# Chunked linear attention in front of a two-layer pair: eight heads to a step instead of four, two accumulator banks for the first product, and the split of the weights on another engine

## Chip, cores and metric

The kernel runs on one core of one Trainium2 chip. The metric is the device time of one execution in microseconds; three runs of the kernel before gave a median of 1195.69 us (1194.02 to 1195.76). TensorE is PE in the tables (its weight loads PEld), VectorE is DVE, ScalarE is ACT, GpSimd is POOL, SyncE is SP and issues the DMAs.

## Reference

The inputs q, k and v have 4 batches, 8 heads, 768 positions and 64 features. The weights are two pairs of a 512 x 2048 and a 2048 x 512 matrix. All of it is float32 for the result; the weights reach the chip as float64 words.

```python
gamma = 1.0 - 2.0 ** (-5.0 - np.arange(H, dtype=np.float32))
for t in range(S):
    state = gamma[None, :, None, None] * state + np.einsum('bhd,bhe->bhde', k[:, :, t], v[:, :, t])
    y[:, :, t] = scale * np.einsum('bhd,bhde->bhe', q[:, :, t], state)
x = y as 3072 tokens x 512
h = x @ w_in;  x = np.maximum(0.01 * h, h) @ w_out        # first pair
h = x @ w_in2; out = np.where(h > 0, h, exp(min(h, 0)) - 1) @ w_out2   # second pair
```

## The kernel before, in words

The 3072 tokens are 24 chunks of 128 positions (six to a batch) and 6 blocks j of 512 tokens (four chunks to a block). The hidden width 2048 is 16 slices m of 128. A step is one slice for one block. It consists of a first product h = w_in[m] x (L225, 12 matmuls), the nonlinearity on ACT (`leaky`, L304), its split into a high and a low part (`split_g`: ACT L231, then DVE or POOL L232), and a second product into four accumulators y (L246, 12 matmuls, issued two steps later by `drain`). Each product is three matmuls per operand pair, since every operand is held as a rounded high part and a remainder (hi·hi, hi·lo, lo·hi). There are 96 steps for each of the two pairs, so 384 blocks of 12 matmuls. Their order is written out by hand in `VISITS` (L46): block 0 with slices 0 to 3, block 1 with slices 0 to 7, block 0 with the other 12, block 1 with the other 8, then whole blocks. A visit that does not finish its 16 slices stores its accumulators to memory, and the later visit adds them (`drain`, L270 to L280).

Attention works on units of half a chunk, four heads (`att_a`, `att_b`; 48 units). One unit does: scores sc = k·q (L357), a mask product to SBUF on DVE (pt, L363 and L365), then into one bank o the state part st·q (L382), pt·v (L385) and the state's increment k·v (L389); ACT copies the output to xhi (L392), DVE updates the state st (L398, two instructions, or L401) and writes the remainder xlo (L402). POOL scales k and q by the decay tables (`prep_k` L333, `prep_q` L342). These matmuls are plain float32, and the profile shows each as two records, so a unit has eight records for each of the four kinds. `att_step` (L418) issues the scores of the next unit and the outputs of the present one together. Eight units stand ahead of the first step, two go with each of the next four steps, then they are spread thinly over blocks 2 to 5's waiting time.

PSUM has eight banks: y takes four, h one, the scores two, o one. One unit in two of the first four chunks uses the y banks instead.

The first pair's weights arrive as 16 loads of 1 MB in 64-bit words (`load_w`) and are converted in the kernel, one slice at a time, by a list of operations (`conv_ops`): ACT takes the top 16 bits out (`put`, L93), DVE masks them twice (`c_exp`, L96 and L97), ACT rebiases the exponent (L100), DVE builds the mantissa (`c_top` L103, `c_low` L107), joins the sign (`c_sign` L111) and multiplies (`c_mul` L114). Then `c_split` rounds to the high part on ACT and forms the remainder on POOL (`halves`, L117 and L118). `conv(n)` issues the next n of these operations; the loop over steps (L461) says how many. The second pair's weights are converted during blocks 2 to 5 in the same way by `pre`, and go through memory.

All DMAs are issued by SP in program order. The first ones are chunk 0, the tables, weight 0, then chunks 1 to 5 with weights 1 to 3 between them. Inside the loop a step issues the load of chunk c+2 and of the next weight.

```python
# the loop of a step, shortened
gemm1(0, m, j % 2, h); conv(n1); gf = leaky(h)
if n > 2: att_step(3 if s < 2 else 2)
else: c_split()
split_g(s, gf, nc.gpsimd if vi < 2 else nc.vector, gp, 3)
drain(s - 2, ...); conv(n2)
if n > 2: att_step(1, 1)
```

Of the kernel before, what the change touches and what calls it, by code (L numbers as in the profile page):

```python
# [19 lines left out]
F32 = mybir.dt.float32  # L20
# [11 lines left out]
P = 128  # L32
# [20 lines left out]
def body(ctx: ExitStack, tc: tile.TileContext, kkv, w1, w2, tabs, out):  # L53
# [19 lines left out]
    raw, wt, cvt, exps, ready = {}, {}, {}, [], []  # L73
# [42 lines left out]
    def halves(hi, lo, f):  # L116
        nc.scalar.copy(hi, f)  # L117
        nc.gpsimd.tensor_tensor(lo, f, hi.bitcast(F32), ALU.subtract)  # L118

# [23 lines left out]
    def c_mul(i):  # L143
        e, _, f = cvt.pop(i)
        power(e, f)
        ready.append((i, f))

    def c_split():
        if ready:
            i, f = ready.pop(0)  # L150
            t = wt[0, i] = wp.tile([P, 2 * W], F32R, tag=f"w{i}", name="w")
            halves(t[:, :W], t[:, W:], f)

    def conv_ops():
        yield c_put, 0
        for i in range(MF):
            yield c_exp, i
            yield c_top, i
            yield c_low, i
            yield c_sign, i  # L160
            if i + 1 < MF:
                yield c_put, i + 1
            yield c_mul, i

# [28 lines left out]
    def pre(more):  # L193
# [20 lines left out]
        halves(r[:, :BLK], r[:, BLK:], f)  # L214
# [93 lines left out]
    with ExitStack() as actx:  # L308
# [4 lines left out]
        st = ab.tile([P, NP, D], F32, name="st")  # L313
        tab = ab.tile([P, H * C + NP * C + 2 * H], F32, name="tab")
        ktab = tab[:, :H]
        mask = tab[:, H : H + H * C].rearrange("p (i r t) -> p i r t", i=2, r=2)
        qtab = tab[:, H + H * C : H + H * C + NP * C].rearrange("p (a t) -> p a t", a=NP)
        gtab = tab[:, H + H * C + NP * C :]
# [10 lines left out]
        def prep_k(w):  # L329
            c, i = divmod(w, 2)  # L330
            if c < NCH and c % NCB < NCB - 1:
                k = kv[c][:, 2, 4 * i * D : 4 * (i + 1) * D].rearrange("p (h d) -> p h d", h=4)
                nc.gpsimd.tensor_tensor(k, k, ktab[:, 4 * i : 4 * i + 4].unsqueeze(2).to_broadcast([P, 4, D]), ALU.mult)  # L333

        qd = {}

        def prep_q(w):
            c, i = divmod(w, 2)
            if c < NCH and c % NCB:
                qd[w] = ap_.tile([P, 2, C], F32, tag="qd", name="qd", bufs=3)  # L340
                q = kv[c][:, 1, 2 * i * C : 2 * (i + 1) * C].rearrange("p (a t) -> p a t", a=2)
                nc.gpsimd.tensor_tensor(qd[w], q, qtab[:, 2 * i : 2 * i + 2, :], ALU.mult)  # L342

        def att_a(w):


            c, i = divmod(w, 2)
            if w < 2 * CPB and i:
                sc = [ps.tile([P, 2 * C], F32, tag=f"y{r}", name="sc") for r in range(2)]
            else:  # L350
                both = aps.tile([P, 2, BLK], F32, tag="s", name="sc")[:, :, : 2 * C]
                sc = [both[:, r] for r in range(2)]
            for p in range(2):
                a = slice((2 * i + p) * C, (2 * i + p + 1) * C)
                for r in range(2):
                    rs = slice(r * D, (r + 1) * D)
                    nc.tensor.matmul(sc[r][:, p * C : (p + 1) * C], kv[c][rs, 0, a], kv[c][rs, 1, a], start=True, stop=True,  # L357
                                     skip_group_check=True)
            yield
            t = ap_.tile([P, 2, 2 * C], F32, tag="pt", name="pt")  # L360
            if w < 2 * CPB and i:
                for r in range(2):
                    nc.vector.tensor_tensor(t[:, r], sc[r], mask[:, i, r], ALU.mult)  # L363
            else:
                nc.vector.tensor_tensor(t, both, mask[:, i], ALU.mult)  # L365
            pt[w] = t
            yield

        def att_b(w):

            c, i = divmod(w, 2)
            cb = c % NCB
            t = pt.pop(w)
            if w < 2 * CPB and i:
                o = ps.tile([P, 2, 2, C], F32, tag="y2", name="o")
            else:
                o = aps.tile([P, 2, 2, C], F32, tag="o", name="o")
            pairs = [(p, 2 * i + p, r, slice(r * D, (r + 1) * D)) for p in range(2) for r in range(2)]
            if cb:
                q = qd.pop(w)  # L380
                for p, a, r, rs in pairs:
                    nc.tensor.matmul(o[rs, p, 0, :], st[rs, a, :], q[rs, p, :], start=(p == 0), stop=False, skip_group_check=True)  # L382
            for p, a, r, rs in pairs:
                v = kv[c][:, 3, a * C + r * D : a * C + (r + 1) * D]
                nc.tensor.matmul(o[rs, p, 0, :], v, t[:, r, p * C : (p + 1) * C], start=(cb == 0 and p == 0), stop=True, skip_group_check=True)  # L385
            if cb < NCB - 1:
                for p, a, r, rs in pairs:
                    hs = slice(a * C + r * D, a * C + (r + 1) * D)
                    nc.tensor.matmul(o[rs, p, 1, :D], kv[c][:, 2, hs], kv[c][:, 3, hs], start=False, stop=True, skip_group_check=True)  # L389
            b, ts = c // CPB % 2, slice(c % CPB * C, (c % CPB + 1) * C)  # L390
            ks = slice(2 * i, 2 * i + 2)
            nc.scalar.copy(xhi[b][:, ks, ts], o[:, :, 0, :])  # L392
            yield
            if cb < NCB - 1:
                if cb:
                    for p in range(2):
                        a = 2 * i + p
                        nc.vector.scalar_tensor_tensor(out=st[:, a, :], in0=st[:, a, :], scalar=gtab[:, a : a + 1],  # L398
                                                       in1=o[:, p, 1, :D], op0=ALU.mult, op1=ALU.add)
                else:  # L400
                    nc.vector.tensor_copy(st[:, ks, :], o[:, :, 1, :D])  # L401
            nc.vector.tensor_tensor(xlo[b][:, ks, ts], o[:, :, 0, :], xhi[b][:, ks, ts].bitcast(F32), ALU.subtract)  # L402
            yield

        NU = 2 * NCH
# [5 lines left out]
        load_w()  # L411
        nc.sync.dma_start(out=tab[:, cut:], in_=tabs[:, cut:])
        for c in range(1, CPB + 2):
            att_load(c)
            if c != 2 and c < CPB + 1:
                load_w()

        def att_step(before=0, between=0):  # L418


            nonlocal au
            w = au
            c, i = divmod(w, 2)
            scores = att_a(w + 1) if w + 1 < NU else iter((0, 0))
            outputs = att_b(w)
            next(scores)
            conv(before)
            next(scores)
            prep_q(w + 2)
            next(outputs)  # L430
            conv(between)
            next(outputs)
            prep_k(w + 1)
            c_split()
            if i and CPB <= c < NCH - 2:
                att_load(c + 2)
            au += 1
# [7 lines left out]
        au = 0  # L445
# [4 lines left out]
        for _ in att_a(0):  # L450
            pass
        for w, (n1, n2) in enumerate(((0, 1), (0, 1), (1, 0), (1, 1), (0, 1), (1, 1), (0, 1), (1, 1))):
            att_step(n1, n2)
            if w < 2:
                warm(1)


        units = {0: 4, 3: 2, 4: 1, 5: 1, 6: 1}
        pace = {1: (2, 2), 2: (2, 1)}
        NA = next(s for s, (_, j, _, _) in enumerate(steps) if j == NB - 1)  # L460
        for s in range(NA):  # L461
            ph, j, m, (_, _, m0, m1, vi) = steps[s]
            n = units.get(vi, 0)
            h = ps.tile([P, BLK], F32, tag="h", name="h")
            gemm1(0, m, j % 2, h)
            n1, n2 = pace.get(vi, (0, 0))
            conv(n1)
            gf = leaky(h)
            if n > 2:
                att_step(3 if s < 2 else 2)  # L470
            else:
                c_split()
            split_g(s, gf, nc.gpsimd if vi < 2 else nc.vector, gp, 3)
            drain(s - 2, stage_w if vi < 2 or m < m0 + 2 and vi == 2 else stage_f)
            conv(n2)
            if n > 2:
                att_step(1, 1)
            elif n > 1 or n and m % 2:
                att_step()
# [87 lines left out]
def _tables():  # L567
# [9 lines left out]
    tab[:, :H] = ktab.T  # L577

    mask = mask.reshape(2, 2, 2, C, C).transpose(3, 0, 2, 1, 4)
# [3 lines left out]
    tab[:, H + H * C + NP * C :][:, :NP] = np.repeat(gamma.reshape(NP, 2) ** C, D, axis=1).T  # L583
    return tab


# [33 lines left out]
```

## Time and profile before

| | |
|---|---|
| median of three runs | 1195.69 us (1194.02 to 1195.76) |
| the profiled execution | 1194.88 us, span 1193.1 us, mean granted TensorE clock 0.991 of full speed |
| PE busy | 1165.4 us, 98% of the span, 6024 matmul records |
| DVE, ACT, POOL busy | 661.4 us (55%), 544.6 us (46%), 166.0 us (14%) |
| DMA | 117.11 MB, mean 98 GB/s |
| chain that ended last | PE 87%, DVE 7%, ACT 2%, DMA 2% |

A matmul's recorded duration overlaps the next one's, so PE's busy time is read as time in which it was not idle, and speed is read from the starts of consecutive instructions. Starts are microseconds from the first instruction of the program.

### The profile page before, as it was taken

The page shows a single profiled execution, that of the slowest core. Times are in us where ns is not written, and L with a number is a line of the kernel's source. Part 1 is how long each engine was busy: PE and PEld are TensorE (multiplying, and loading weights), DVE is VectorE, ACT ScalarE, POOL GpSimd, SP SyncE. Part 2 cuts the span into 40 slices and gives each one's busy share as a digit, 9 for nine tenths or more (in the row PEclk, how much of TensorE's full clock was granted, in tenths as well). Part 3 has the DMA queues.
Part 4 walks back from the last instruction along what each step waited for, and adds up shares of the span by engine and source line. Part 5 has one row for each costly group of instructions (what it writes and reads, how often), then busy time and mean ns, then how long its engine had stood idle before and what let it go on. Part 6 is the DMA issues. An engine that isn't in the chain of part 4 may idle for free.

```text
span 1193.1 us, 15132 instructions
## 1 busy us (share of the span) xinstructions
PE 1165.4 (98%) x6024; PEld 945.0 (79%) x6024; DVE 661.4 (55%) x1081; ACT 544.6 (46%) x913; POOL 166.0 (14%) x145
## 2 busy tenths in 40 slices
PE   7798999999999999999999999999999999999998
PEld 4576778778888777778888888888888888888887
DVE  5969861324653564453211566666666665666665
ACT  2355532223453444353222555565555555555554
POOL 4565420111331223031000000000000000000000
PEclk9899999999999999999999999999999999999999
DMA  9266120324553464351355600000010010000000
GB/s 377 75 246 246 35 71 1 106 107 141 195 194 124 177 212 158 135 195 61 106 176 191 232 18 18 36 18 18 36 34 2 36 36 1 36 1 1 36 1 36
DMA packets 32822, 117.11 MB, mean 98 GB/s; under 512 B 3184, under 2 KB 3184, under 8 KB 25712
## 3 DMA queue, kind: packets, MB, share of 16 engines
q1 hardware_dynamic: 32752, 116.15, 27.0%
q8 instruction: 47, 0.77, 0.3%
q14 instruction: 23, 0.19, 0.1%
HBM read 84.68 MB, written 31.46 MB: 97 GB/s over the span
## 4 chain that ended last, share of the span: by engine, by line
PE 87%; DVE 7%; ACT 2%; DMA 2%; issue 1%; SPq 0%; ACTq 0%; DVEq 0%
PE h L225 41%; PE y L246 40%; PE sc L357 2%; PE o L385 2%; PE o L382 2%; DMA raw<-in_w 1%; DVE s L96 1%; DVE f L114 1%; DVE f L107 1%; DMA kv<-in_kkv 1%; DVE glo L232 1%; DVE e L111 1%; PE o L389 1%; DVE e L97 1%; ACT w L117 0%
## 5 line engine op out<-in xcount | busy, mean ns | idle before, releaser
L225 PE MATMUL h<-xhi,w 128*128 128x512 f32 x1536 | 512.5, 395 | 6.9 <-ACT gf L304 6.9
L232 DVE TENSOR_TENSOR glo<-gf,ghi 128x512 fp32r<-128x512 f32 x180 | 134.7, 749 | 429.3 <-ACT ghi L231 425.3
L225 PEld LDWEIGHTS h<-xhi,w 128*128 128x128 f32 x1536 | 290.0, 189 | 74.6 <-ACT gf L304 10.7
L225 PE MATMUL h<-xlo,w 128*128 128x512 f32 x768 | 301.2, 392 | 1.6 <-DVE xlo L402 1.6
L246 PE MATMUL y<-ghi,w 128*128 128x512 f32 x768 | 252.4, 390 | 1.5 <-DVE ysb L279 1.5
L246 PE MATMUL y<-w,ghi 128*128 128x512 f32 x768 | 236.4, 389 | 0.0
L246 PEld LDWEIGHTS y<-ghi,w 128*128 128x128 f32 x768 | 144.2, 188 | 32.2 <-DVE ysb L279 2.0
L225 PEld LDWEIGHTS h<-xlo,w 128*128 128x128 f32 x768 | 145.2, 189 | 30.8 <-DVE xlo L402 2.0
L246 PEld LDWEIGHTS y<-w,ghi 128*128 128x128 f32 x768 | 144.2, 188 | 30.0
L515 ACT ACTIVATE n<-h 128x512 f32<-128x512 f32 x96 | 57.4, 598 | 224.4 <-PE h L225 224.4
L246 PE MATMUL y<-glo,w 128*128 128x512 f32 x384 | 149.4, 389 | 0.0
L246 PE MATMUL y<-w,glo 128*128 128x512 f32 x384 | 149.4, 389 | 0.0
L304 ACT ACTIVATE gf<-h 128x512 f32<-128x512 f32 x96 | 57.1, 594 | 164.1 <-PE h L225 164.0
L231 ACT CAST ghi<-gf 128x512 fp32r<-128x512 f32 x192 | 117.7, 613 | 6.0 <-DVE gf L526 3.4
L246 PEld LDWEIGHTS y<-w,glo 128*128 128x128 f32 x384 | 72.0, 188 | 14.9
L246 PEld LDWEIGHTS y<-glo,w 128*128 128x128 f32 x384 | 72.1, 188 | 14.8
L100 ACT ACTIVATE e<-e,ebias 128x512 int16<-128x512 uint16 (+1 forms) x48 | 41.5, 865 | 64.3 <-DVE e L97 64.3
L523 DVE SCALAR_TENSOR_TENSOR a<-n,a 128x512 f32<-128x512 f32 x96 | 65.6, 683 | 5.9 <-ACT n L518 5.9
L525 DVE SCALAR_TENSOR_TENSOR t<-a,t 128x512 f32<-128x512 f32 x96 | 66.5, 692 | 3.3
L526 DVE SCALAR_TENSOR_TENSOR gf<-h,t 128x512 f32<-128x512 f32 x96 | 66.4, 691 | 3.3
L118 POOL TENSOR_TENSOR raw<-f,raw 128x512 fp32r<-128x512 f32 x32 | 41.1, 1284 | 188.8 <-ACT raw L117 162.2
L524 DVE SCALAR_TENSOR_TENSOR t<-n,t 128x512 f32<-128x512 f32 x96 | 65.7, 684 | 0.0
(48 smaller groups left out, 933.1 us busy)
## 6 DMA issues: line engine op xcount, KB each, us to landing
kv<-in_kkv SPq DMA_DIRECT2D x23, 1024.0 KB, 5.5
raw<-in_w SPq DMA_DIRECT2D x16, 1024.0 KB, 9.6
raw<-in_w SPq DMA_DIRECT2D x32, 512.0 KB, 3.5
wscr<-raw SPq DMA_DIRECT2D x32, 512.0 KB, 3.0
w<-wscr SPq DMA_DIRECT2D x16, 1024.0 KB, 4.8
xs<-yscr SPq DMA_DIRECT2D x12, 512.0 KB, 3.9
out<-osb SPq DMA_DIRECT2D x24, 256.0 KB, 4.0
yscr<-ysb SPq DMA_DIRECT2D x16, 256.0 KB, 2.8
```

Of the source, the lines that this page charges most:

```text
L100: nc.scalar.activation(e.bitcast(I16), e, AF.Relu, bias=ebias, scale=2.0**3)
L118: nc.gpsimd.tensor_tensor(lo, f, hi.bitcast(F32), ALU.subtract)
L225: nc.tensor.matmul(h, a, x, start=(n == 0), stop=(n == 3 * KD - 1))
L231: nc.scalar.copy(ghi, gf)
L232: eng.tensor_tensor(glo, gf, ghi.bitcast(F32), ALU.subtract)
L246: nc.tensor.matmul(acc[d], lhsT, rhs, start=(first and n == 0), stop=(last and n == 2))
L304: nc.scalar.activation(gf, h, AF.Prelu, alpha=0.01)
L515: nc.scalar.activation(n, h, AF.Relu, scale=-1.0)
L523: nc.vector.scalar_tensor_tensor(out=a, in0=n, scalar=1.0, in1=a, op0=ALU.add, op1=ALU.mult)
L524: nc.vector.scalar_tensor_tensor(out=t, in0=n, scalar=1.0, in1=t, op0=ALU.add, op1=ALU.mult)
L525: nc.vector.scalar_tensor_tensor(out=t, in0=a, scalar=2.0, in1=t, op0=ALU.add, op1=ALU.mult)
L526: nc.vector.scalar_tensor_tensor(out=gf, in0=h, scalar=0.0, in1=t, op0=ALU.max, op1=ALU.add)
```

## The change

Attention goes by whole chunks (eight heads): `scores`, `masked`, `outputs`, `states`. Scores and outputs share one tile x of two banks; the outputs of a chunk go to both banks, and the head pair of bank k with half r is written to partition half r xor k, for which the rows of the first weight matrix are reordered on the way in. Inside `outputs` the order is pt·v, k·v, then st·q. q is scaled in place once its scores are done. The state is multiplied by the decay into sg ahead of time and added in one instruction. h alternates between two banks, h and z. The four accumulators are two tiles of two banks. The remainders of the weights are formed on DVE, in the list of `conv_ops`, one operation behind the next slice's masks. First visits have 5, 8, 11 and 8 slices. The remainder of g goes to POOL only in the first visit (before: the first two), and there `drain` runs one step behind instead of two. Outputs stand behind the first product of a step, scores behind the second product of the step before (blocks 1 and 2) or of two steps before (blocks 3 to 5). The first loads are chunk 0, the tables, chunk 1, weight 0, chunk 2, chunk 3, weight 1, chunk 4, weight 2, chunk 5, weight 3.

```diff
-    [(0, 0, 4), (1, 0, HM), (0, 4, MF), (1, HM, MF)] + [(j, 0, MF) for j in range(2, NB)],
+    [(0, 0, V0), (1, 0, HM), (0, V0, MF), (1, HM, MF)] + [(j, 0, MF) for j in range(2, NB)],
+V0 = CPB + 1
 def c_mul(i):
-    ready.append((i, f))
-def c_split():
-        halves(t[:, :W], t[:, W:], f)
+    nc.scalar.copy(t[:, :W], f)
+    ready[i] = f
+def c_split(i):
+    nc.vector.tensor_tensor(t[:, W:], ready.pop(i), t[:, :W].bitcast(F32), ALU.subtract)
 def conv_ops():
             yield c_exp, i
+            if i:
+                yield c_split, i - 1
...
-                acc = [ps.tile([P, BLK], F32, tag=f"y{d}", name=f"y{d}") for d in range(4)]
+                both = [ps.tile([P, 2, BLK], F32, tag=f"y{i}", name=f"y{i}") for i in range(2)]
+                acc = [both[d // 2][:, d % 2] for d in range(4)]
...
+        def outputs(c, pool, tag):
+            places = [(i, k, 2 * i + k, r) for i in range(2) for k in range(2) for r in range(2)]
+            by_column = [(i, k, 2 * i + k, x ^ k) for i in range(2) for k in range(2) for x in range(2)]
+            for i, k, a, r in by_column:
+                nc.tensor.matmul(o[half(r ^ k), k, pair(i)], v, t[:, r, pair(a)], start=(i == 0), stop=True, skip_group_check=True)
+                for i, k, a, r in places:
+                    nc.tensor.matmul(o[half(r), k, 2 * C + i * D : 2 * C + (i + 1) * D], kv[c][:, 2, hs], kv[c][:, 3, hs],
+                                     start=False, stop=True, skip_group_check=True)
+                for i, k, a, r in places:
+                    nc.tensor.matmul(o[half(r ^ k), k, pair(i)], st[half(r), 2 * k + i, :], kv[c][half(r), 1, pair(a)],
+                                     start=False, stop=True, skip_group_check=True)
+            nc.scalar.copy(x[0], y)
+        def states(c, o, x, y):
+                    nc.vector.tensor_tensor(n, m, o[:, :, 2 * C : 2 * C + 2 * D], ALU.add)
+            nc.vector.tensor_tensor(x[1], y, x[0].bitcast(F32), ALU.subtract)
+                nc.vector.tensor_tensor(sg, st, gtab.unsqueeze(2).to_broadcast([P, NP, D]), ALU.mult)
...
+        sc1 = scores(1, aps, "x"); prep(1); masked(1, sc1, wp, "w10")
+        sc2 = scores(2, ps, "y0"); prep(2); conv(3)
+        o1 = outputs(1, ps, "y1"); masked(2, sc2, wp, "w9"); conv(2); states(1, *o1)
+        sc3 = scores(3, aps, "x"); prep(3); masked(3, sc3, wp, "w10")
+        o2 = outputs(2, ps, "y0"); conv(2); states(2, *o2)
+        o3 = outputs(3, ps, "y1"); states(3, *o3); conv(1)
...
+        pace = {0: (2, 2, 2), 1: (2, 1, 1), 2: (2, 1, 0)}
+            h = (aps if s % 2 else ps).tile([P, BLK], F32, tag="z" if s % 2 else "h", name="h")
+            gemm1(0, m, j % 2, h); conv(n1); gf = leaky(h)
+            if c is not None:
+                o = outputs(c, aps, "x"); conv(n2); states(c, *o)
+                if c < NCH - 2: att_load(c + 2)
+            else: conv(n2)
+            split_g(s, gf, nc.gpsimd if vi < 1 else nc.vector, gp, 3)
+            drain(s - (1 if vi < 1 else 2), ...)
+            c = sc_at.get(s)
+            if c is not None:
+                sc = scores(c, aps, "x"); prep(c); masked(c, sc, ap_, "pt")
+            conv(n3)
```

Lines are joined here where the change has them one below the other; a line of "..." marks what is left out.

## Rows read from the trace of the kernel before

**Rows 1.** The page: length of the profiled span, and the number of instructions.

```profile
span 1193.1 us, 15132 instructions
```

**Rows 2.** Timeline of PE: start us, us, engine line; first matmuls of consecutive blocks.

```profile
84.26 0.39 PE L225 MATMUL h<-xhi,w 128*128 128x512 f32 x1
...
86.98 0.39 PE L246 MATMUL y<-ghi,w 128*128 128x512 f32 x1
```

**Rows 3.** Timeline of PE: one attention unit, the block after it, the next unit's beginning.

```profile
219.85 0.72 PE L357 MATMUL sc<-kv 64*128 64x128 f32 x8
220.50 0.65 PE L382 MATMUL o<-qd,st 64*64 64x128 f32 x8
221.08 0.66 PE L385 MATMUL o<-pt,kv 128*64 128x128 f32 x8
221.57 0.40 PE L389 MATMUL o<-kv 128*64 128x64 f32 x8
221.90 0.50 PE L225 MATMUL h<-xhi,w 128*128 128x512 f32 x1
...
224.79 0.39 PE L246 MATMUL y<-ghi,w 128*128 128x512 f32 x1
...
227.60 0.60 PE L357 MATMUL sc<-kv 64*128 64x128 f32 x6
```

**Rows 4.** Three stretches: length, then PE, PEld, DVE, ACT, POOL busy, granted clock, DMA.

```profile
34.85:78.65 43.80, 36.95 (x301) 27.96 (x297) 36.20 (x52) 18.95 (x27) 25.83 (x19) 0.88 0.38 145
78.65:200.00 121.35, 113.61 (x490) 91.87 (x487) 81.53 (x80) 56.68 (x76) 44.84 (x23) 0.99 0.31 113
200.00:575.00 375.00, 374.26 (x2278) 298.61 (x2277) 171.98 (x371) 141.02 (x244) 79.21 (x81) 1.00 0.41 144
```

**Rows 5.** Timeline of PE: a block's first matmul, and the last block's last.

```profile
196.09 0.39 PE L246 MATMUL y<-ghi,w 128*128 128x512 f32 x1
...
1189.09 0.39 PE L246 MATMUL y<-w,glo 128*128 128x512 f32 x1
```

**Rows 6.** Waits from 78.65 to 200 us: total us, times, longest us.

```profile
PE h L225 <- ACT gf L304: 6.2, 5, 1.9
...
PE y L246 <- DVE ysb L279: 1.5, 1, 1.5
```

**Rows 7.** Timeline of DVE: one weight slice's conversion, with POOL idle until 84.59.

```profile
81.03 0.42 DVE L96 TENSOR_SCALAR s<-e 128x1024 uint16<-128x1024 uint16 x1
...
81.82 0.69 DVE L103 TENSOR_SCALAR f<-raw 128x1024 uint32<-128x1024 uint32 x1
...
82.54 1.23 DVE L107 SCALAR_TENSOR_TENSOR f<-f,raw 128x1024 f32<-128x1024 uint32 x1
...
83.68 0.68 DVE L111 TENSOR_TENSOR e<-e,s 128x1024 uint16<-128x1024 uint16 x1
...
84.40 1.22 DVE L114 SCALAR_TENSOR_TENSOR f<-f,e 128x1024 f32<-128x1024 f32 x1
```

**Rows 8.** Timeline of POOL and DVE at 71 us.

```profile
70.91 2.38 POOL L118 TENSOR_TENSOR w<-f,w 128x1024 fp32r<-128x1024 f32 x1 [2.55 <-ACT w L117]
70.98 2.86 DVE L103 TENSOR_SCALAR f<-raw 128x1024 uint32<-128x1024 uint32 x1
```

**Rows 9.** Groups by line: busy us, mean ns of one, idle before and its releasers.

```profile
L118 POOL TENSOR_TENSOR w<-f,w 128x1024 fp32r<-128x1024 f32 x16 | 42.4, 2650 | 64.7 <-ACT w L117 51.7 <-PE h L225 6.0 <-PE sc L357 3.5
...
L342 POOL TENSOR_TENSOR qd<-kv,tab 128x256 f32<-128x256 f32 x40 | 38.0, 950 | 101.1 <-DMA kv<-in_kkv 57.7 <-PE o L382 43.5
...
L365 DVE TENSOR_TENSOR pt<-sc,tab 128x512 f32<-128x512 f32 x44 | 30.1, 684 | 28.5 <-PE sc L357 22.8 <-DMA tab<-in_tabs 5.6
...
L232 POOL TENSOR_TENSOR glo<-gf,ghi 128x512 fp32r<-128x512 f32 x12 | 18.6, 1550 | 8.0 <-issue 3.8 <-ACT ghi L231 3.7 <-POOL glo L232 0.5
```

**Rows 10.** Timeline at the start: the first uses of chunks 1 and 2.

```profile
13.62 1.22 PE L357 MATMUL sc<-kv 64*128 64x128 f32 x8 [3.67 <-DMA kv<-in_kkv]
...
18.51 0.73 POOL L342 TENSOR_TENSOR qd<-kv,tab 128x256 f32<-128x256 f32 x1 [1.88 <-DMA kv<-in_kkv]
```

More of the change, by code (lines that the diff above doesn't have):

```diff
@@ L344, in att_a @@
[L344 to L354, printed above, removed]
-                for r in range(2):
[L356 to L367, printed above, removed]
@@ L369, in att_b @@
-        def att_b(w):
-            c, i = divmod(w, 2)
-            cb = c % NCB
[L373 to L378, printed above, removed]
-            if cb:
[L380 to L385, printed above, removed]
-            if cb < NCB - 1:
[L387 to L394, printed above, removed]
@@ new lines, in scores, with masked @@
+        def scores(c, pool, tag):
+            sc = pool.tile([P, 2, BLK], F32, tag=tag, name="sc")
+            for a in range(NP):
+                for r in range(2):
+                    nc.tensor.matmul(sc[:, r, pair(a)], kv[c][half(r), 0, pair(a)], kv[c][half(r), 1, pair(a)],
+                                     start=True, stop=True, skip_group_check=True)
+            return sc
+        def masked(c, sc, pool, tag, bufs=1):
+            t = pt[c] = pool.tile([P, 2, BLK], F32, tag=tag, name="pt", bufs=bufs)
+            nc.vector.tensor_tensor(t, sc, mask, ALU.mult)
@@ L395, in att_b @@
+        def states(c, o, x, y):
+            cb = c % NCB
+            if cb < NCB - 1:
+                n = st.rearrange("p (k i) d -> p k (i d)", k=2)
+                m = sg.rearrange("p (k i) d -> p k (i d)", k=2)
                 if cb:
[L396 to L399, printed above, removed]
-                else:
-                    nc.vector.tensor_copy(st[:, ks, :], o[:, :, 1, :D])
@@ L414, in body @@
             att_load(c)
-            if c != 2 and c < CPB + 1:
+            if c != 2:
                 load_w()
[L418 to L437, printed above, removed]
         def warm(n):
@@ L449, in body @@
         prep_k(0)
[L450 to L459, printed above, removed]
+        sc0 = scores(0, ps, "y0")
+        masked(0, sc0, wp, "w9")
+        o0 = outputs(0, ps, "y1")
+        warm(1)
+        states(0, *o0)
+        sc1 = scores(1, aps, "x")
+        prep(1)
+        masked(1, sc1, wp, "w10")
+        sc2 = scores(2, ps, "y0")
+        prep(2)
+        conv(3)
+        o1 = outputs(1, ps, "y1")
+        masked(2, sc2, wp, "w9")
+        conv(2)
+        states(1, *o1)
+        sc3 = scores(3, aps, "x")
+        prep(3)
+        masked(3, sc3, wp, "w10")
+        o2 = outputs(2, ps, "y0")
+        conv(2)
+        states(2, *o2)
+        o3 = outputs(3, ps, "y1")
+        states(3, *o3)
+        conv(1)
+        out_at, sc_at = {}, {}
+        first = {vi: min(s for s, x in enumerate(steps) if x[3][4] == vi and x[0] == 0) for vi in range(len(VISITS[0]))}
+        for i in range(CPB):
+            out_at[1 + i], sc_at[i] = CPB + i, CPB + i
+            out_at[first[3] + 2 * i], sc_at[first[3] + 2 * i - 1] = 2 * CPB + i, 2 * CPB + i
+            for vi in range(4, len(VISITS[0]) - 1):
+                out_at[first[vi] + 4 * i], sc_at[first[vi] + 4 * i - 2] = (vi - 1) * CPB + i, (vi - 1) * CPB + i
+        pace = {0: (2, 2, 2), 1: (2, 1, 1), 2: (2, 1, 0)}
         NA = next(s for s, (_, j, _, _) in enumerate(steps) if j == NB - 1)
@@ L577, in _tables @@
     tab[:, :H] = ktab.T
-    mask = mask.reshape(2, 2, 2, C, C).transpose(3, 0, 2, 1, 4)
+    mask = mask.reshape(NP, 2, C, C).transpose(2, 1, 0, 3)
     tab[:, H : H + H * C] = mask.reshape(P, H * C)
```

96 lines of the change are left out of this document (53 added, 43 removed).

## The prediction

> **What bounds the kernel now.** I read the page first, for the span [rows 1], then PE's timeline block by block, then busy time by stage, then the waits. A block of 12 matmuls lasts 86.98 - 84.26 = 2.72 us where nothing disturbs it [rows 2], and there are 384 of them: 1044.5 us. Nothing in the change shortens that. What can go is the rest, 148.6 us of the 1193.1 us span [rows 1]. It lies in four places.
>
> 1. The opening and the first visit, up to 78.65 us, where the window of the next stage begins [rows 4]. By then 6 blocks are done (4 first products, 2 second ones). From 34.85 on PE is busy for 36.95 of 43.80 us at a mean granted clock of 0.88, so a part of it ran at 1.2 GHz, and DVE is busy for 36.20 us and POOL for 25.83 us of the same stretch [rows 4].
> 2. From 78.65 to 196.09 us [rows 4, 5]: 39 blocks, 106.1 us undisturbed, in 117.4 us. So 11.3 us are lost. PE waits five times, 6.2 us in all and 1.9 us at the longest, for ACT to free the single bank of h, and 1.5 us for an accumulator [rows 6]; the rest is the slower blocks around those waits (each wait also shows on the next matmuls).
> 3. From 196.09 to 1189.3 us, where the last matmul's successor would start [rows 5]: 339 blocks, 922.1 us, in 993.2 us. The 71.1 us above that are the last 16 chunks' attention and under 2 us of other losses. PE is busy for 374.26 of 375.00 us there [rows 4]: it is work, not waiting.
> 4. A tail of 3.8 us after the last matmul [rows 1, 5]. It stays.
>
> **The price of attention, and the first gain.** One unit costs PE 221.90 - 219.85 = 2.05 us for its four streams (0.65, 0.58, 0.49, 0.33), 0.17 us because the block after it takes 2.89 instead of 2.72, and 0.09 us because the block before it ends later (224.79 to 227.60 is 2.81): 2.31 us, so 4.62 per chunk [rows 2, 3]. A chunk has the same matmuls after the change, but in longer streams. The window cut at 228 us shows six records of a stream in 0.60 us where eight take 0.72: a further pair of records costs 0.72 - 0.60, which is 0.11 to 0.12 with the rounding; I take 0.11 [rows 3]. Sixteen scores then cost 0.65 + 4 x 0.11 = 1.09, pt·v 0.49 + 0.44 = 0.93, k·v (half as many columns, so half the pair) 0.33 + 0.22 = 0.55, st·q 0.58 + 0.44 = 1.02 us. The two places where a chunk now interrupts the blocks cost 2 x 0.26. Sum 4.11, so 0.5 us less per chunk and 8.0 us over 16 chunks. Bounds: the joints between st·q, scores and the large matmuls are not in the trace in the new order; if each joint cost what the dearest one shows (0.2 us more per chunk) the gain is 5, and if none cost anything it is 12.
>
> In st·q the change puts the four products of a step on four different pairs of a row half and a column half. Every stream of the trace advances by two records at a time, whatever its shape [rows 3], and I keep that. The Trainium skill, TensorEngine Tiling (Array Packing), section Tiling Modes, states otherwise for this case: a 64x64 configuration is four independent tiles, which can work at once. By that page the sum below would be some 8 us lower; it is a rival.
>
> **The opening.** Chunk 1 is first used at 13.62 us and chunk 2 at 18.51, both on landing, with one weight load between them: 2.45 us per MB [rows 10]. The weight 0 that lay ahead of chunk 1 now lies behind it, so chunk 1 comes at 11.1, weight 0 at 13.6, chunk 2 at 16.0, chunk 3 at 18.5, weight 1 at 20.9. PE takes scores(2) before outputs(1), so outputs(1) wait for chunk 2 and run from 17.2 to 19.7. Then DVE sets the pace, by the durations of rows 7: sign and multiply to 21.5 (POOL holds it up once), states(1) to 23.0, mask(3) to 24.2, the next exponent and the remainder of weight 0 to 26.3, the state of chunk 2 to 26.7; PE's st·q of chunk 3 ends at 27.6, ACT's copy at 28.2, DVE's xlo at 29.3. The first product starts at about 29 instead of 34.85 [rows 4].
>
> **The first visit.** A weight costs DVE 0.79 for both masks, then 0.69, 1.23, 0.68 and 1.22, so 4.6 us [rows 7], and now 1.22 more for the remainder (a two-operand pass over 128x1024 as L114). A chunk costs one mask at 1.22 (two at 0.684 before [rows 9]), xlo 0.68, and two passes over 256 elements at 0.42 (0.684 less the 0.54 per 512 between the two sizes, halved): 2.74. That is 8.6 us per step. POOL blocks DVE: an L103 that takes 0.69 alone took 2.86 beside a 2.38 us L118 [rows 7, 8]. In each step before, POOL had L118 at 2.65, one g remainder at 1.55 and four decays of some 0.95 or less [rows 9]; after, one g remainder and two decays of some 1.3 (bounds 0.95 and 1.9, one or two narrow ones), so 4.2 at most. The step's PE work is two blocks and a chunk, 9.6 us. What it cannot hide: the remainder of the next weight stands on DVE behind the mask of the next scores, and the next first product needs it for its third matmul; so 1.22 + 1.22 - 0.45 = 2.0 us in each of four steps. New waits, then, with all of PE's queue behind them. Sum up to 5 first and 4 second products with 8 chunks: 29.0 + 9 x 2.72 + 4 x 4.11 + 4 x 2.0 = 78.0, and 0.5 for the clock. The kernel before reaches the same work at 78.65 + 3 x 2.72 = 86.8. Gain 8.3. Bounds: none at all, even 3 us of loss, if DVE and POOL add up fully as 8.6 + 4.2 us in every step and PE falls to 1.2 GHz; 13 if the clock holds and the remainder finds room.
>
> **The middle.** With two banks, ACT may free h 5.4 us later than now before PE waits; the longest wait was 1.9 [rows 6]. POOL is then free of L118 and of g's remainder, so nothing blocks DVE: four list entries of 0.98 and g's remainder at 0.68 are 4.6 us in a step of 5.44. Its slack of 0.8 us is the new cover; if it goes, the remainder of a weight is late next, and PE waits for that as in the first visit. The accumulators in pairs: the first matmul of a visit now waits for two copies, and the block of first products before it (2.72 us) covers them; at the worst another 1.5 us wait [rows 6]. I take 2.0 us of loss in place of 11.3: gain 9.3, bounds 3 (only the second half of POOL's blocking goes) and 11.3.
>
> **Costed at nothing.** The loads of chunks and weights are as many as before and issued by SP in the same step, with a chunk's load now ahead of `split_g`; DMA is 31 to 41% busy there [rows 4]. Wider decays on POOL in blocks 2 to 5 delay DVE by up to 1.3 us each, twice per chunk; DVE is busy for 172 of 375 us there [rows 4], and a chunk's scores lie two to four blocks ahead of its outputs. The second pair's part is unchanged.
>
> **Sum.** 1194.88 - 8.3 - 9.3 - 8.0 = 1169.3 us for the profiled execution, which stands 0.8 under the median of the runs shown: 1170.
>
> **Rivals.**
> - Four products at once in st·q. Its 16 records then take some 0.45 us less, in 14 of the last 16 chunks 6.3 us and with the earlier ones about 8: 1162. For it: disjoint halves and disjoint banks. Against it: no row has more than two together [rows 3]. It is what the Array Packing page of the Trainium skill gives.
> - The second bank doesn't do what it says. If ACT is late because DVE feeds it late (the waits for gf are only the last link), PE then waits for g or for a weight's remainder instead, and the middle keeps its loss: 1179. For it: DVE busy for 81.53 of 121.35 us in that stretch [rows 4]. Against it: a part of that busy time was waiting for POOL [rows 8].
> - Slower: one x tile. Scores, mask, outputs and states now hand the same two banks on one by one, and PE's queue stands still at each handover that DVE doesn't finish within one block, 2.72 us. There are 40 handovers after the opening. It decides from the point where DVE comes more than 3.4 us after scores or outputs: 40 x 0.7 = 28 us eat the 26 us gained; at 4 us late in each it is 40 x 1.28 = 51 us, so 1221, and 1196 if only half of them are so late. For it: DVE takes 36.20 of 43.80 us in the first visit. Against it: only 46% of the later stretch [rows 4], where 32 of the 40 lie.
>
> **The numbers.** 1170 by the sum, chance 0.56 (its own range 1163 to 1177). Four at once 0.18, the middle's loss kept 0.16, with the first visit's gain also lost up to 1187. The slower case 0.05. The last 0.05 are other mixes, 0.02 of them within 0.2% of the time before. A measurement of this kernel can tell 0.2%, 2.4 us. The range 1157 to 1184 takes in the first three cases and most of their bounds and leaves out the slower one. Faster 0.93, same 0.02, slower 0.05.
>
> **What would show it.** The first product at about 29 us; scores of 16 records in about 1.1 us and st·q in about 1.0 (0.55 under the first rival); no wait of PE for gf; in the first visit PE waiting four times some 2 us for DVE's remainder of w; POOL without the weights' rows and DVE's L103 back at 0.69. It is wrong if the middle's 39 blocks still take over 114 us, if a chunk in blocks 3 to 5 still adds 4.6 us, or if PE's waits in the first visit come to over 15 us.

## The result and the profile after

The changed kernel takes 1168.39 us (median of four, 1165.39 to 1169.17) beside 1195.25 us of the kernel before on the same chip: a ratio of 0.977, 95% interval 0.975 to 0.979. The profiled execution took 1167.77 us. One run of the experiment with one bank, 2462.54 us, is slow beyond comparison, and all times below are medians without it.

The page and three stretches of its trace, which answer to [rows 1] and [rows 4] (columns as there):

```profile
span 1166.0 us, 14854 instructions
...
PE 1140.8 (98%) x6022; PEld 932.5 (80%) x6022; DVE 653.0 (56%) x1016; ACT 541.7 (46%) x889; POOL 102.3 (9%) x82
```

```profile
29.03:80.81 51.78, 42.66 (x332) 31.73 (x333) 42.28 (x51) 22.66 (x29) 14.41 (x10) 0.93 0.41 156
80.81:183.74 102.93, 99.85 (x433) 82.14 (x432) 71.96 (x91) 52.46 (x69) 3.82 (x2) 0.98 0.33 119
183.74:1161.50 977.76, 977.76 (x5013) 803.39 (x5011) 520.43 (x851) 456.62 (x781) 74.90 (x58) 1.00 0.25 87
```

The cuts are those of the prediction: the first product starts at 29.03, five first and four second products and eight chunks are done at 80.81, 45 blocks at 183.74, and 1161.50 is where the last matmul's successor would start. POOL is busy for 3.82 us of the middle, where the kernel before had 44.84 us in the stretch of [rows 4].

| stage | before | after | gain | predicted |
|---|---|---|---|---|
| nine blocks and eight chunks done at | 86.8 | 80.81 | 6.0 | 8.3 |
| the next 36 blocks: loss (before: 39 blocks) | 11.3 | 5.0 | 6.3 | 9.3 |
| 339 blocks: time above 2.72 us each | 71.1 | 55.7 | 15.4 | 8.0 |
| tail | 3.8 | 4.5 | -0.7 | 0 |

The 86.8 is the prediction's own (78.65 + 3 blocks; the trace has 86.98). A loss is the stretch less 2.72 us for each of its blocks (102.93 - 97.9 = 5.0; 977.76 - 922.1 = 55.7). The four rows add up, but for the rounding, to the 27.1 us between the spans. The sum that was forecast, 25.6, is nearly met, but one term is almost twice its forecast and two fall short.

PE's waits in the changed kernel over the whole span (total us, times, longest us), beside [rows 6]:

```profile
PE h L226 <- DVE w L149: 7.2, 4, 2.2
PE sc L354 <- DMA kv<-in_kkv: 3.7, 1, 3.7
PE y L247 <- ACT ysb L281: 3.1, 1, 3.1
PE o L372 <- DVE pt L360: 2.1, 2, 1.3
```

No wait for gf is left, and none of these lies behind 100 us. One chunk of block 3 on PE's timeline, which answers to [rows 3]:

```profile
288.94 1.16 PE L354 MATMUL sc<-kv 64*128 64x128 f32 x16
290.03 0.50 PE L226 MATMUL h<-xhi,w 128*128 128x512 f32 x1
...
292.89 0.39 PE L247 MATMUL y<-ghi,w 128*128 128x512 f32 x1
...
298.42 1.09 PE L372 MATMUL o<-pt,kv 128*64 128x128 f32 x16
299.35 0.63 PE L376 MATMUL o<-kv 128*64 128x64 f32 x16
299.91 0.67 PE L380 MATMUL o<-kv,st 64*64 64x128 f32 x16
300.51 0.50 PE L247 MATMUL y<-ghi,w 128*128 128x512 f32 x1
...
303.38 0.39 PE L226 MATMUL h<-xhi,w 128*128 128x512 f32 x1
```

From start to start: scores 1.09 us, pt·v 0.93, k·v 0.56, st·q 0.60. The blocks behind take 2.86 and 2.87 us, and the two ahead end 0.09 late each, so the joints cost 0.47. Together 3.65 us, against 4.62 before and 4.11 forecast. All terms but st·q are within 0.05 us of the forecast; st·q was put at 1.02.

### The profile page after: what moved, and what is told of

It is laid out like the page before. It is cut to its first block, busy times and chain, and to the rows that moved or that the text cites. A ratio compares the mean times of both kernels' runs of the same rounds, so it can differ in the third digit from the quotient of the medians.

```text
span 1166.0 us, 14854 instructions
## 1 busy us (share of the span) xinstructions
PE 1140.8 (98%) x6022; PEld 932.5 (80%) x6022; DVE 653.0 (56%) x1016; ACT 541.7 (46%) x889; POOL 102.3 (9%) x82
## 4 chain that ended last, share of the span: by engine, by line
PE 94%; DVE 3%; DMA 1%; ACT 0%; SPq 0%; issue 0%; DVEq 0%
PE y L247 45%; PE h L226 44%; PE sc L354 2%; PE o L372 2%; DMA kv<-in_kkv 1%; PE o L380 1%; DVE w L149 1%; PE o L376 1%; DVE pt L360 1%; DVE f L108 0%; DVE f L115 0%; DVE f L104 0%; DVE e L112 0%; DVE xlo L397 0%; DVE e L98 0%
## 5 line engine op out<-in xcount | busy, mean ns | idle before, releaser
L233 DVE TENSOR_TENSOR glo<-gf,ghi 128x512 fp32r<-128x512 f32 x187 | 130.3, 697 | 382.4 <-ACT ghi L232 380.5
L247 PE MATMUL y<-ghi,w 128*128 128x512 f32 x768 | 256.0, 394 | 3.1 <-ACT ysb L281 3.1
L522 ACT ACTIVATE t<-n 128x512 f32<-128x512 f32 x96 | 60.7, 632 | 3.1
```

What stands on the lines that cost most here:

```text
L233: eng.tensor_tensor(glo, gf, ghi.bitcast(F32), ALU.subtract)
L247: nc.tensor.matmul(acc[d], lhsT, rhs, start=(first and n == 0), stop=(last and n == 2))
L522: nc.scalar.activation(t, n, AF.Tanh, scale=-0.5)
```

## Experiments

All but the last are the changed kernel with the edit shown. "Middle" and "later blocks" are the second and third row of the table. In the profiles of kernels that keep the opening, the first product starts between 28.3 and 29.8 us, and once, in the last run of the line of edits, at 32.09; so differences below about 1.5 us there are not read. The runs were made on several chips, on which the kernel before took 1194.15 to 1196.33 us (medians); a ratio is against the same chip, and differences of about 1 us between times of different experiments are not read. A loss is read from one profile each.

**Four at once in st·q, by order.** The first run only brings the four products of one bank, on two combinations of halves, ahead of the other four.

```diff
-                for i, k, a, r in places:
+                for i, k, a, r in sorted(places, key=lambda x: x[1]):
```

> The changed kernel with st·q in another order: first the four products whose head pair goes to bank 0, then the four of bank 1, so that neighbours use only two of the four pairs of row half and column half. Theory (four products on four different pairs of halves run together): a stream of 16 records goes back from 0.60 us to 1.0 or a little less, 0.4 us in each of the 19 chunks that have st·q outside the opening's waits, so 7 to 8 us more than the changed kernel's 1168.4. Rival (st·q is short because it is one long stream and has nothing to do with the halves): 0.60 us stays, and the time stays within 1 us.

Measured: 1168.26 us (ratio 0.977, 0.975 to 0.978), st·q 0.61 us, where it was 0.60. The order inside the stream is worth next to nothing. On PE's timeline of this run:

```profile
301.55 0.68 PE L380 MATMUL o<-kv,st 64*64 64x128 f32 x16
302.16 0.50 PE L247 MATMUL y<-ghi,w 128*128 128x512 f32 x1
```

This doesn't speak against four at once if the later products can start beside the earlier ones in this order too, which is an argument and not seen in a row; the theory's expectation was wrong in any case. So the combinations themselves were reduced to two (lines shortened):

```diff
-                matmul(o[half(r ^ k), k, pair(i)], v, ...)
+                matmul(o[half(r), k, pair(i)], v, ...)
-                    matmul(o[half(r ^ k), k, pair(i)], st[half(r), 2 * k + i, :], ...)
+                    matmul(o[half(r), k, pair(i)], st[half(r), 2 * k + i, :], ...)
-        w[:, k][:, [k, 1 - k]]
+        w[:, k][:, [0, 1]]
```

> The outputs of both banks stay in the half of their own head, so the state part st·q uses two combinations of a row half and a column half in place of four; banks, records and sizes are as in the changed kernel. Theory (four different combinations are worked on at once): with two combinations the 16 records of st·q advance two at a time again and take 0.95 to 1.05 us instead of 0.60; 14 of the last 16 chunks and some six before them pay 0.4 us each, so 1174 to 1177 us. Rival (the stream is short because it writes two banks, or because long streams are cheap in general): st·q stays at 0.60 us and the time within 1.5 us of 1168.4.

Measured: 1176.58 us (ratio 0.984, 0.982 to 0.986). The same place on PE's timeline:

```profile
305.60 1.09 PE L380 MATMUL o<-kv,st 64*64 64x128 f32 x16
306.62 0.50 PE L247 MATMUL y<-ghi,w 128*128 128x512 f32 x1
```

st·q takes 1.02 us, the very figure of the prediction's sum. The later blocks take 5.8 us more, which is 14 chunks by 0.42. Banks, records and sizes are the same (the halves that pt·v writes change too, but it takes 0.92 us here and 0.93 in the changed kernel), so the four different pairs of a row half and a column half make the stream short.

**One bank for h.**

```diff
-            h = (aps if s % 2 else ps).tile([P, BLK], F32, tag="z" if s % 2 else "h", name="h")
+            h = ps.tile([P, BLK], F32, tag="h", name="h")
```

> The changed kernel with a single bank for h. Theory (the second bank takes away PE's waits for ACT): waits of PE for gf come back, 4 to 6 us of them with the slower blocks around them between 80 and 185 us, and some in the first visit; 1173 to 1176 us. Rival (the waits went because nothing of POOL blocks DVE any more, so ACT is no longer late): no such waits, within 1 us of 1168.4.

Measured: 1177.84 us (median of three; ratio 0.985, 0.983 to 0.986), so the bank is worth some 9.5 us, more than the theory had. The later blocks lose 9.1 more, and the middle 5.2 instead of 5.0. PE's waits of this run in the middle (81.59 to 184.70 us), then from 200 to 575 us:

```profile
PE h L226 <- ACT gf L306: 3.8, 3, 1.6
...
PE h L226 <- ACT gf L306: 7.1, 7, 1.7
```

In the middle the waits for gf did come back, near the theory's size, but the wait of 3.1 us for a copy of the accumulators, which the changed kernel has there, is gone, and the granted clock stayed at 1.00 (0.98 there). So the 0.2 us is the difference of two kinds of waits. ACT's timeline in the later blocks:

```profile
453.41 0.72 ACT L101 ACTIVATE e<-e,ebias 128x512 int16<-128x512 uint16 x1 [2.86 <-DVE e L98]
455.66 0.62 ACT L214 CAST raw<-f 128x512 fp32r<-128x512 f32 x1 [1.53 <-DVE f L115]
456.19 0.59 ACT L306 ACTIVATE gf<-h 128x512 f32<-128x512 f32 x1
```

ACT stands in the conversion of the second pair, waiting for DVE, and the leaky that would free h stands behind it. The kernel before had one bank too and 0.7 us of such waits in all its later blocks; the new order needs the second bank there.

**The weights' remainders on POOL.**

```diff
-        nc.vector.tensor_tensor(t[:, W:], ready.pop(i), t[:, :W].bitcast(F32), ALU.subtract)
+        nc.gpsimd.tensor_tensor(t[:, W:], ready.pop(i), t[:, :W].bitcast(F32), ALU.subtract)
```

> The changed kernel with the remainders of the first pair's weights on POOL again (128x1024, at their new place in the list). Theory (what counts is that POOL's 2.4 to 2.65 us block DVE): DVE instructions beside them take 2 to 3 us, PE's four waits for the remainder of w in the first visit grow from 1.8 to some 3.5 us each, and the middle loses 3 to 6 us more; 1175 to 1185 us. Rival (DVE's own 1.22 us is as dear as being blocked): within 2 us of 1168.4, or faster.

Measured: 1189.41 us (ratio 0.995, 0.993 to 0.996). The nine blocks are done at 100.66 instead of 80.81, the middle loses 6.7, the later blocks are the same. A wait of PE, then POOL and DVE in this run:

```profile
PE h L226 <- POOL w L149: 22.4, 4, 9.2
```

```profile
56.08 1.28 POOL L233 TENSOR_TENSOR glo<-gf,ghi 128x512 fp32r<-128x512 f32 x1 [10.32 <-ACT ghi L232]
57.32 1.27 POOL L341 TENSOR_TENSOR kv<-kv,tab 128x512 f32<-128x512 f32 x1
58.55 2.79 POOL L149 TENSOR_TENSOR w<-f,w 128x1024 fp32r<-128x1024 f32 x1
...
59.17 3.25 DVE L108 SCALAR_TENSOR_TENSOR f<-f,raw 128x1024 f32<-128x1024 uint32 x1
```

The operation on DVE that takes 1.23 us alone [rows 7] takes 3.25 beside POOL's 2.79. Nearly all of the 21 us lies in the first visit, whose granted clock also fell from 0.93 to 0.81; without this part 6.5 us would be left of the change. Neither side had this size: the theory expected waits of 3.5 us each (measured 5.6 on the mean) and 3 to 6 us more loss in the middle (measured 1.6). PE waits for POOL itself here, whose remainder starts only behind g's remainder and the scaling of q; how much of the price is that queue and how much is DVE held up beside it stays open. It is measured in the new order of operations only.

**The remainder's matmuls last.** In visit 0 the first product takes its eight matmuls with the high part of w before its four with the remainder.

```diff
+        if last:
+            order = [t for trio in trios for t in trio[:2]] + [trio[2] for trio in trios]
...
-            gemm1(0, m, j % 2, h)
+            gemm1(0, m, j % 2, h, vi == 0)
```

> The changed kernel with the first visit's first products in another order: the eight matmuls with the high parts of w first, the four with its remainder last, so that the remainder is needed 1.8 us later than now. Theory (the four waits of 1.8 us for the remainder cost PE 7.2 us and some 4 us of slower blocks behind them): no wait of PE for the remainder, the first visit ends 5 to 9 us earlier, 1160 to 1163 us. Rival (DVE paces the first visit: 8.6 us of its own work and POOL's on top against 9.7 of PE): the wait moves to the mask, to the state or to the accumulator's operands, and the gain is below 3 us.

Measured: 1164.55 us (ratio 0.974, 0.973 to 0.976), between the two. The nine blocks are done 4.8 us earlier, at 76.00, of which 0.7 is an earlier start (28.34) and 4.1 the visit; the middle gives back 1.3. So the waits for the remainder did not vanish, they were more than halved, and PE waits 1.5 us for POOL's scaling of q in the visit instead. PE's waits (lines 3 higher):

```profile
PE y L250 <- ACT ysb L284: 4.1, 1, 4.1
...
PE h L229 <- DVE w L149: 3.3, 3, 1.4
```

**The first loads in the old order.**

```diff
+        load_w()
         nc.sync.dma_start(out=tab[:, cut:], in_=tabs[:, cut:])
         for c in range(1, CPB + 2):
             att_load(c)
-            if c != 2:
+            if c != 2 and c < CPB + 1:
```

> The changed kernel with weight 0 loaded ahead of the second table part and of chunk 1, as before the change; the same loads in all. Theory (the prediction's: chunk 2's landing releases the outputs of chunk 1, and the opening's gain is the order of the loads): chunks 1 to 3 land 2.4 us later, the first product starts at 31.0 to 31.7 instead of 29.03 and the time rises by 2 to 3 us. Rival (DVE's work sets the first product's start, the loads have room): 28.7 to 29.5 us, and the time within 1 us of 1168.4.

Measured: 1170.49 us (ratio 0.980, 0.979 to 0.981). On PE's timeline:

```profile
13.32 1.16 PE L354 MATMUL sc<-kv 64*128 64x128 f32 x16 [2.61 <-DMA kv<-in_kkv]
...
31.11 0.51 PE L226 MATMUL h<-xhi,w 128*128 128x512 f32 x1 [0.70 <-ACT xhi L385]
```

Chunk 1 comes at 13.32 as in [rows 10] (10.97 in the changed kernel) and the first product at 31.11, 2.1 us after the changed kernel's. The order of the loads is 2.1 of the opening's 5.8 us (34.85 to 29.03), with the spread above 1.3 to 2.8; time and start are as the theory had them.

From the first product on its code is the changed kernel's, and it shows what one profile's loss is worth. PE waits 3.1 us for the same copy of the accumulators, but the block behind that wait takes 102.15 - 99.30 = 2.85 us here and 4.46 in the changed kernel's profile, and the middle loses 3.4 us and not 5.0:

```profile
99.30 0.50 PE L247 MATMUL y<-ghi,w 128*128 128x512 f32 x1 [3.08 <-ACT ysb L281]
...
102.15 0.39 PE L226 MATMUL h<-xhi,w 128*128 128x512 f32 x1
```

The granted clock is 1.00 throughout this middle; behind the same wait it fell in one profile and not in the other.

**The copies of visit 0's accumulators.** The wait of 3.1 us at 94.94 us looks as follows on ACT and DVE in the changed kernel:

```profile
90.10 1.15 ACT L101 ACTIVATE e<-e,ebias 128x1024 int16<-128x1024 uint16 x1 [1.63 <-DVE e L98]
91.16 0.58 ACT L306 ACTIVATE gf<-h 128x512 f32<-128x512 f32 x1
...
94.30 1.19 ACT L281 COPY ysb<-y 128x512 f32<-128x512 f32 x2 [1.91 <-DVE ysb L281]
```

```profile
91.84 1.23 DVE L108 SCALAR_TENSOR_TENSOR f<-f,raw 128x1024 f32<-128x1024 uint32 x1
92.98 0.68 DVE L233 TENSOR_TENSOR glo<-gf,ghi 128x512 fp32r<-128x512 f32 x1
93.58 1.28 DVE L281 COPY ysb<-y 128x512 f32<-128x512 f32 x2
```

ACT copies half of each tile, and waits 1.91 us for DVE, which has the other half and is late with its list. The edit gives ACT the first tile and DVE the second:

```diff
-                (nc.scalar.copy if d % 2 else nc.vector.tensor_copy)(t, acc[d])
+                (nc.scalar.copy if (d < 2 if ph == 0 and j == 0 else d % 2) else nc.vector.tensor_copy)(t, acc[d])
```

> The changed kernel with the four accumulators of visit 0 copied pair by pair: ACT takes both halves of the first tile, DVE both of the second. Theory (the next visit's first matmul waits for two copies, one of which stands on DVE behind the list of weight operations): the wait of 3.1 us at the accumulators falls to 1.5 us or less and the middle's loss from 5.0 to about 3.3 us; the time falls by 1.5 to 2 us. Rival (ACT itself is late there, since its own work waits for DVE): the wait stays at 2.5 to 3.5 us and the time within 0.7 us of 1168.4.

Measured: 1164.98 us (ratio 0.976, 0.974 to 0.978); the middle loses 2.7 instead of 5.0, and two waits for copies of 1.9 us in all (1.6 the longer) are left. The time fell by 3.4 us where the theory had 1.5 to 2, though by the ratios of the two kernels, each to its own chip, by 1.7, with intervals that overlap. Of the middle's 2.3 us, 1.6 is the clock that fell in the changed kernel's profile and not in this one; against the run with the old order of loads the pairwise copies are worth 0.7.

**The edits together, and one step less of lag.** The third edit of the first run below puts `leaky` ahead of `conv(n1)` from visit 1 on.

> Three edits on the changed kernel together: in visit 0 the matmuls with the weight's remainder stand last in the first product, the copies of visit 0's accumulators go pair by pair, and from visit 1 on ACT's leaky stands ahead of the list of weight operations. Theory (each removes a wait of its own): 3.8 us from the first as measured, 1.5 to 2 from the second, up to 1 from the third: 1161 to 1163 us. Rival (what is saved early in the first visit is waited for later, since DVE's sum of work is the bound there): 1164 to 1166 us, no better than the first edit alone.

Measured: 1161.90 us (ratio 0.973, 0.971 to 0.974), as the theory had it; the middle loses 3.4 us, no less than with the old order of loads, with one wait for the copies of 2.6. The next run lets the second product of the fifth step come one step earlier:

```diff
-            drain(s - (1 if vi < 1 else 2), ...)
+            drain(s - (1 if vi < 1 or s == V0 else 2), ...)
```

> The kernel of three edits with the second products one step behind, in place of two, in the first step of visit 1 also: two first products (5.4 us) then stand between the last product into visit 0's accumulators and the next visit's first one, in place of one. Theory (the 2.6 us wait for the copies is short of cover only): the wait falls below 0.8 us, the middle's loss from 3.4 to 1 us or less, the time to 1158 to 1160 us. Rival (ACT and DVE are behind by their sum of work there, and the wait returns at g or at a weight's remainder): the middle's loss stays above 2.5 us and the time is 1161 to 1163 us.

Measured: 1160.07 us (ratio 0.969, 0.968 to 0.971), the fastest of all. The time is the upper end of the theory's range; the middle's loss, 2.2 us, lies between the two sides, and the wait that is left (1.4 us, again for copies) stands ahead of a block at 132.29 us, behind visit 1. The last run of this line takes back the place of `leaky`:

> As the run with the shorter lag, but ACT's leaky stands behind the list of weight operations again, as in the changed kernel. Theory (with two banks for h, ACT's leaky has 5 us of room, so its place is worth nothing): within 0.8 us of the run with the shorter lag. Rival (behind the list ACT waits for DVE's masks before it can free h, and the middle pays for it): 1 to 3 us slower, with waits of PE for gf or ghi in the middle.

Measured: 1162.77 us (ratio 0.973, 0.970 to 0.975), 2.7 us slower: the rival's size, though the waits that it named are hardly in the profile (0.3 us for gf), so the cause is open. The profiled execution, at 1168.35 us, was the longest of the four (the others 1162.12 to 1162.96), so its stretches are not compared.

**Two parts undone together.** One bank for h and the remainders on POOL, the two edits above.

> Two parts of the change undone together: one bank for h, and the weights' remainders on POOL. Undone singly they cost the middle 0.2 and 1.6 us. Theory (each of the two removes the cause of the waits for h by itself: POOL that blocks DVE makes ACT late, and the second bank forgives it): undone together the middle's loss rises to 10 to 13 us, about that of the kernel before, and PE waits for gf there again; in all 1198 to 1204 us, above the sum of the two alone. Rival (the middle's gain comes from neither, but from the first visit of five slices and the weights that are then already converted): the costs only add up, the middle's loss stays below 8 us, and the time is 1197 to 1200 us with first visit and later blocks as in the two single runs.

Measured: 1199.64 us (ratio 1.002, 1.001 to 1.003), a time that fits both expectations. The middle loses 9.0 us, which fits neither. PE's only waits there:

```profile
PE h L226 <- ACT gf L306: 4.7, 3, 3.4
```

Singly the two cost the middle 0.2 and 1.6 us, together 4.0. The mean granted clock of the middle is 1.00, 0.98 and 0.97 in these three runs and 0.98 in the changed kernel, so a part of these differences is where the clock fell.

**One part alone in the kernel before.**

```diff
-            split_g(s, gf, nc.gpsimd if vi < 2 else nc.vector, gp, 3)
+            split_g(s, gf, nc.gpsimd if vi < 1 else nc.vector, gp, 3)
```

> The kernel before with one part of the change alone: from visit 1 on the remainder of g is formed on DVE instead of POOL (eight steps move). With both suspected causes of the middle's loss put back into the changed kernel, it lost 9.0 us there and the kernel before 11.3. Theory (what is left between the two is g's remainder on POOL, which blocks DVE in visit 1): the loss from 78.65 us on, over the next 39 blocks, falls from 11.3 to 8.5 to 9.5 us and the time to about 1193 us, 2 us less. Rival (POOL's remainders of the weights block DVE in either case, and DVE only gets more to do): the loss stays at 10.5 us or more and the time is within 1 us of the kernel before, or above it.

Measured: 1206.26 us (ratio 1.009, 1.007 to 1.010), against the theory and on the rival's dearer side. The 39 blocks behind the first visit, from 77.02 us on:

```profile
77.02:206.23 129.21, 113.47 (x473) 90.56 (x469) 82.01 (x88) 55.80 (x74) 30.23 (x16) 0.96 0.29 106
```

They lose 129.21 - 106.1 = 23.1 us, twice the 11.3 of before, though DVE and POOL together are busy for 112 us here and for 126 us in the stretch of [rows 4]. PE's waits there:

```profile
PE h L225 <- ACT gf L304: 10.3, 5, 4.1
PE y L246 <- DVE ysb L279: 5.4, 2, 3.9
```

My reading, not tried apart: with POOL still at the weights' remainders, the remainder of g stands in DVE's queue behind operations that POOL holds up, and what ACT waits for comes later. What is shown is that this move alone costs 11 us in the kernel before; whether it is worth anything inside the change no run here shows.

## Why the prediction came out right

**The time** came out at 1168.39 where 1170 was forecast, by a sum whose terms were wrong in both directions and happened to cancel: that it came within 2 us is luck.

**The chunks** are the mis-sized term. The step that failed is "Every stream of the trace advances by two records at a time, whatever its shape, and I keep that": st·q took 0.60 us for 16 records instead of 1.02. The rival's mechanism held, at the 0.45 us a chunk that it named (0.42). The Trainium skill, TensorEngine Tiling (Array Packing), Tiling Modes, says that different tiles can execute in parallel; the two st·q runs agree with it. The rows of before could not tell: their st·q used two combinations only. Of the 15.4 us, 14 x 0.42 = 5.9 are st·q, 8.0 the longer streams and joints as forecast, and 0.7 the waits for gf that the kernel before had there; 0.8 is not assigned. The run with two combinations bears this out: without four at once it keeps 9.6 of the 15.4. The rival's time of 1162 needed the sum's other terms too, and they fell short.

**The opening** came as forecast: first product at 29.03 for "about 29", by the landing of chunk 2 in part (2.1 us); the other 3.7 were not tried apart. Chunk 2 was forecast at 16.0:

```profile
15.88 2.08 PE L354 MATMUL sc<-kv 64*128 64x128 f32 x16 [3.74 <-DMA kv<-in_kkv]
```

The outputs of chunk 1 ended at 21.3 and not at 19.7, with a granted clock of 0.50 from 16 to 20 us; the chain behind them made that up.

**The first visit** ends at 80.81, not 78.5. "Four waits of 2.0 us" for a weight's remainder are four waits of 7.2 us in all, so that term held. A wait of 1.3 us for the high part of weight 1 from ACT was not in the sum. DVE's L104 (L103 before) was back at 0.68 to 0.69 us in three of the five slices; beside POOL's remainder of g and its scaling of q it still took 1.78 and 1.77. What failed is the "0.5 for the clock". PE's timeline in the second step and in the fourth, and three stretches, the last of them in the middle:

```profile
38.09 1.05 PE L226 MATMUL h<-xhi,w 128*128 128x512 f32 x2
38.94 0.63 PE L226 MATMUL h<-xlo,w 128*128 128x512 f32 x1
39.37 1.05 PE L226 MATMUL h<-xhi,w 128*128 128x512 f32 x2
...
60.01 0.50 PE L226 MATMUL h<-xhi,w 128*128 128x512 f32 x1
60.35 0.40 PE L226 MATMUL h<-xlo,w 128*128 128x512 f32 x1
62.69 0.73 PE L226 MATMUL h<-xhi,w 128*128 128x512 f32 x2 [1.94 <-DVE w L149]
...
65.17 1.09 PE L372 MATMUL o<-pt,kv 128*64 128x128 f32 x16
```

```profile
38.00:41.00 3.00, 3.00 (x8) 1.97 (x6) 2.97 (x3) 0.00 (x0) 3.00 (x3) 0.50 0.00 0
52.00:54.50 2.50, 2.50 (x13) 1.66 (x13) 2.43 (x5) 0.56 (x1) 0.00 (x0) 0.50 0.00 0
96.00:99.00 3.00, 3.00 (x8) 2.30 (x7) 2.65 (x4) 2.76 (x4) 0.00 (x0) 0.50 1.14 289
```

Three matmuls from 38.09 to 39.37 take 0.427 us each, where 2.72 / 12 = 0.227 is the undisturbed pace: TensorE runs at 1.2 GHz behind the first two of these waits, where its granted clock is 0.50. The four later first products take 5.93, 6.42, 5.16 and 5.16 us on the timeline; above four blocks and the waits that is 22.67 - 10.88 - 7.2 = 4.6 us. Of it 3.5 are in the two blocks in which the clock fell; the other two, at full clock, lose 0.5 each (65.17 - 60.01 - 2.72 - 1.94). Putting the remainder's matmuls last takes 4.1 us off the 12 for both.

**The middle** lost 5.0 us, where 2.0 were taken. The waits for gf went, as forecast, but the step "the block of first products before it (2.72 us) covers" the two copies failed: 3.1 us of wait, and a block at half the clock behind it (94.94 to 99.40, 4.46 us). The wait comes with this code; the slow block behind it need not, as the run with the old order of loads shows (3.4 us lost with the same wait). The pairwise copies, the shorter lag and the two other edits bring it to 2.2. The sign of being wrong that the prediction gave, over 114 us for 39 blocks, did not come: 36 took 102.93, and three more undisturbed make 111.1. How the gain of 6.3 divides stays open: the second bank alone is worth 0.2 us there and POOL's relief 1.6, together 4.0, and that measure is loose, since in the last of these runs the first visit ended 20 us later and more weights were converted by then. With one bank 3.8 us of waits for gf return in the middle and the wait for the copies goes, so the second bank does take away the waits that it was meant to take, and a wait behind ACT and DVE took their place: in kind that is the second rival's mechanism. The loss that it forecast didn't come; that other parts relieved DVE is the likely reason and is not shown.

**The slower rival** had no part: no wait for pt or o behind 100 us.

## What to carry to other kernels

A sum of terms can be met while half of them are wrong; compare stage by stage, and undo the parts one at a time and in pairs before giving a part its price. Here a stream of small products was short when it used all four pairs of a row half and a column half, in either of two orders; which place an output takes is free if the next weights can be reordered to match. A short wait of PE can cost over half its length again in slower matmuls behind it (here 7.2 us of waits and 4.6 more, most of it where the clock fell), so cover for the operand that comes last is worth a reordering of the product. Whether the clock falls behind a given wait can differ between two profiles of the same stage, so a loss read from a single profile is uncertain by about the length of such a slow block (here 1.6 us).

## What was not expected of the hardware

A stream of 64 x 64 x 128 products on all four pairs of halves took nearly the same time in both orders: 16 records in 0.60 us with banks alternating and in 0.61 with one bank first, where eight on two combinations took 0.58 [rows 3] and 16 on two took 1.02. And the DVE operations shown beside one of POOL are not slower by a share but wait for most of it: 3.25 instead of 1.23 us beside POOL's 2.79 (it ends 62.42 - 61.34 = 1.08 us after POOL's), as 2.86 instead of 0.69 in [rows 7, 8]. The Trainium skill, SBUF — State Buffer, Who interferes with whom, describes that as an exclusive lock between the two engines; these rows agree.
